# A third x tile turned on TensorE at the start, with the first columns of its z brought forward, in a gated mix of linear attention and a spatial MLP

## The chip, the core and the metric

One core of one Trainium2 chip. The metric is the time of one execution in microseconds (us), as the device measures it. A profile of one execution stands beside it: it gives the span from the first to the last instruction, which is a little shorter than the time.

## The reference

For x of 2048 rows and 512 columns the result is a mix of two branches by a gate for each row, all in bf16 with wide sums:

```python
g = _sigmoid((x * gate_w).sum(-1, keepdims=True))
a = _A_ref(x, A_wqkv, A_w_phi, A_wo)     # linear attention, softmax features, 32 heads of 16
b = _B_ref(x, B_w_in, B_w_sp, B_b_sp, B_w_out)
return g * a + (1 - g) * b

def _B_ref(x, w_in, w_sp, b_sp, w_out):
    z = _gelu(jnp.einsum('bsd,df->bsf', x, w_in))      # F = 1376 columns, d = 512
    z1 = z[..., :Fh].copy()
    z2 = _layernorm(z[..., Fh:], axis=-1)
    g = jnp.einsum('ts,bsf->btf', w_sp, z2) + b_sp[None, :, None]
    return jnp.einsum('bsf,fd->bsd', z1 * g, w_out)
```

The change lies in the very first part: x @ w_in, with gate_w carried as one more column of w_in, and the gelu behind it.

## The kernel before

The 2048 rows are 16 tiles of 128 rows. TensorE needs x with its 512 columns on the partitions, as four blocks dt of 128: that is `xT[:, dt, rows]`. For each tile t, z is 1377 columns (1376 of w_in and the gate's column F), done in three pieces, `Z_PIECES` = (0, 512), (512, 1024), (1024, 1377), each a sum over four blocks dt. The three pieces of a tile take three PSUM banks: 0 to 2 for even tiles, 3 to 5 for odd ones (`zbank`). ScalarE then applies gelu to all of the tile's columns in one activation (`z_post`), takes tanh of the gate column, and VectorE takes the layernorm's statistics. Banks 6 and 7 are left for other uses: value projections, the folding of weights, and, at the start, the turning of x.

The order of instructions on each engine is the order of the text (`manual_schedule`); no engine's instructions are reordered against it, and waits between engines come from the data. So the start of the kernel reads as follows.

- `spin(24)` (line 195) runs matmuls on constants into bank 5, while the first loads are on the way. Their results are not used.
- x tiles 0 and 1 are loaded as they are (`xn`, by SP's and ACT's queue), and turned by matmuls with an identity, `x_transpose` (line 201): four 128-column matmuls a tile, into bank 6 for tile 0 and bank 7 for tile 1. `x_copy` brings them from PSUM to `xT` in three parts, for tile 0 on VectorE (line 210), for tile 1 on ScalarE (line 212). `spin(4)` stands behind the transposes.
- w_in is loaded in pieces: columns 0 to 256 (HC) and 256 to 512, each split between SP's and ACT's queue; 512 to 1024 in two halves on SP's; then the rest on SP's. gate_w (`gw`) is loaded on ACT's queue, behind the pieces of w_in and ahead of a one-element gelu.
- z of tiles 0 and 1 is computed in turns of one block each, by columns 0 to 256, 256 to 512 and 512 to 1024. `gate_column` (lines 215 and 218) stands after column 512: a 4-column matmul turns gate_w, and VectorE writes it as column F of w_in. The third piece of both tiles follows.
- Tiles 2 to 15 follow in full, each with its three pieces. x of tiles 2 and 3 comes by one transposing DMA on SP's queue (line 128), of the other tiles by three more. From tile 5 on, projections of v and the folding of weights stand between the tiles.

All z matmuls have line 186. After tile 15 come the features of k and q, the matmuls with w_sp, and the output tiles; the change doesn't touch these.

Of the kernel before, what the change touches and what calls it, by code (L numbers as in the profile page):

```python
# [7 lines left out]
AF = mybir.ActivationFunctionType  # L8
# [3 lines left out]
BF16 = mybir.dt.bfloat16  # L12
I32 = mybir.dt.int32

P = 128
S = 2048
D = 512
H = 32
DH = 16
F = 1376  # L20
# [3 lines left out]
NDT = D // P  # L24
CH = 512
# [15 lines left out]
def kernel(  # L41
# [14 lines left out]
    nc = tc.nc  # L56
    x2 = A_x.flatten_outer_dims()
    out2 = out.flatten_outer_dims()

    pers = ctx.enter_context(tc.tile_pool(name="pers", bufs=1))  # L60
# [5 lines left out]
    ps = psp.tile([P, 8, CH], FP32, name="ps")  # L66

    def zbank(t):
        b = 3 * (t % 2)
        return ps[:, b:b + 3, :].rearrange("p b n -> p (b n)")  # L70

    xT = pers.tile([P, NDT, S], BF16, name="xT")
    w_in = pers.tile([P, NDT, F + 1], BF16, name="w_in")
# [6 lines left out]
    zz = pers.tile([P, NT, F], BF16, name="zz")  # L80
# [6 lines left out]
    wphi = pers.tile([P, NDT, P], BF16, name="wphi")  # L87
    mask16 = pers.tile([P, 8], BF16, name="mask16")
    mask4 = pers.tile([P, 4], BF16, name="mask4")
    xn = pers.tile([P, 2, D], BF16, name="xn")  # L90
    ones = nc.const_aps.tensor(1.0, [P, P], BF16)
    stats = pers.tile([P, NT, 2, 6], FP32, name="stats")
    mv = pers.tile([P, NT, 2], FP32, name="mv")
# [7 lines left out]
    gate = st[:, 2, :]  # L101
    gatem = st[:, 3, :]

    ident = pers.tile([P, P], BF16, name="ident")
    gw = pers.tile([NDT, P], BF16, name="gw")
    nc.gpsimd.memset(ident[:], 1.0)
    nc.gpsimd.affine_select(
        out=ident[:], in_=ident[:], pattern=[[-1, P]],
# [7 lines left out]
    def load_w_in(eng, d0, d1, n0, n1):  # L116
        eng.dma_start(out=w_in[:, d0:d1, n0:n1], in_=w_in_v[:, d0:d1, n0:n1])

    HC = CH // 2
    for n0 in (0, HC):  # L120
        load_w_in(nc.sync, 0, 2, n0, n0 + HC)
        load_w_in(nc.scalar, 2, 4, n0, n0 + HC)
    for d0 in (0, 2):
        load_w_in(nc.sync, d0, d0 + 2, CH, 2 * CH)
    nc.scalar.dma_start(out=gw[:], in_=gate_w.rearrange("(dt p) -> dt p", p=P))
    nc.scalar.activation(out=st[:, 9, 0:1], in_=ones[:, 0:1], func=AF.Gelu_apprx_tanh)
    nc.sync.dma_start(out=w_in[:, :, 2 * CH:F], in_=w_in_v[:, :, 2 * CH:F])
    nc.sync.dma_start_transpose(out=xT[:, :, 2 * P:CH], in_=x2[2 * P:CH, :])
    nc.sync.dma_start(
        out=wv[:, :, :],  # L130
        in_=A_wqkv[:, 2 * D:3 * D].rearrange("(dt p) n -> p dt n", p=P),
    )
    for q in range(1, NCH):
        nc.sync.dma_start_transpose(
            out=xT[:, :, q * CH:(q + 1) * CH], in_=x2[q * CH:(q + 1) * CH, :]
        )
        if q == 1:
            nc.sync.dma_start(
                out=wphiW[:, :, :],
                in_=A_w_phi.rearrange("(g h) e f -> (h e) g f", g=NDT),  # L140
# [3 lines left out]
        out=bcolb[:, :, :], in_=B_b_sp.rearrange("(t p) -> t p", p=P)  # L144
# [7 lines left out]
    for t in range(WSLOTS):  # L152
        load_wsp(t)
    nc.sync.dma_start(
        out=w_out[:, 0:NFT - 1, :],
        in_=B_w_out[0:(NFT - 1) * P, :].rearrange("(ft p) n -> p ft n", p=P),
# [4 lines left out]
        out=w_out[0:last_m, NFT - 1, :], in_=B_w_out[(NFT - 1) * P:FH, :]  # L161
    )
    nc.sync.dma_start(
        out=wo[:, :, :], in_=A_wo.rearrange("(g p) n -> p g n", p=P)
# [4 lines left out]
        out=mask16[:], in_=mask16[:], pattern=[[-16, 8]],  # L169
# [3 lines left out]
        out=mask16[:], in_=mask16[:], pattern=[[16, 8]],  # L173
# [6 lines left out]
    nc.gpsimd.memset(worst[:], 1.0)  # L180
    nc.vector.tensor_tensor(out=mask4[:], in0=mask16[:, 0:4], in1=mask16[:, 4:8], op=ALU.add)

    def z_piece(t, n0, n1, d0=0, d1=NDT):
        zb = zbank(t)
        for dt in range(d0, d1):
            nc.tensor.matmul(  # L186
                zb[:, n0:n1], lhsT=xT[:, dt, t * P:(t + 1) * P], rhs=w_in[:, dt, n0:n1],
                start=(dt == 0), stop=(dt == NDT - 1),
            )

    Z_PIECES = [(0, CH), (CH, 2 * CH), (2 * CH, F + 1)]

    def spin(n):
        for _ in range(n):
            nc.tensor.matmul(  # L195
                ps[:, 5, 0:P], lhsT=ones, rhs=ones, start=True, stop=True
            )

    def x_transpose(t):
        for dt in range(NDT):  # L200
            nc.tensor.matmul(  # L201
                ps[:, 6 + t, dt * P:(dt + 1) * P], lhsT=xn[:, t, dt * P:(dt + 1) * P],
                rhs=ident[:], start=True, stop=True,
            )

    def x_copy(t, d0, d1):
        src = ps[:, 6 + t, :].rearrange("p (d n) -> p d n", d=NDT)
        dst = xT[:, d0:d1, t * P:(t + 1) * P]
        if t == 0:
            nc.vector.tensor_copy(out=dst, in_=src[:, d0:d1, :])  # L210
        else:
            nc.scalar.activation(out=dst, in_=src[:, d0:d1, :], func=AF.Copy)

    def gate_column():
        nc.tensor.matmul(  # L215
            ps[:, 6, 0:NDT], lhsT=gw[:], rhs=ident[0:NDT, 0:NDT], start=True, stop=True
        )
        nc.vector.tensor_copy(out=w_in[:, :, F], in_=ps[:, 6, 0:NDT])

    def z_gelu(t, n0, n1):  # L220
        nc.scalar.activation(  # L221
            out=zz[:, t, n0:n1], in_=zbank(t)[:, n0:n1], func=AF.Gelu_apprx_tanh
        )

    def z_post(t, done=0):
        zb = zbank(t)
        z_gelu(t, done, F)
        nc.scalar.activation(out=gth[:, t:t + 1], in_=zb[:, F:F + 1], func=AF.Tanh, scale=0.5)
        for h in range(2):
            nc.vector.bn_stats(  # L230
                out=stats[:, t, h, :], in_=zz[:, t, FH + h * HF:FH + (h + 1) * HF]
            )
        nc.vector.bn_aggr(out=mv[:, t, :], in_=stats[:, t, :, :].rearrange("p h s -> p (h s)"))
# [43 lines left out]
    def z1_gate(t):  # L277
        nc.vector.tensor_scalar(
            out=zz[:, t, 0:FH], in0=zz[:, t, 0:FH],
            scalar1=gatem[:, t:t + 1], scalar2=None, op0=ALU.mult,  # L280
        )
# [3 lines left out]
    def v_proj(t):  # L285
        b = VBANK.get(t, 6 + t % 2)
        for dt in range(NDT):
            nc.tensor.matmul(  # L288
                ps[:, b, :], lhsT=xT[:, dt, t * P:(t + 1) * P], rhs=wv[:, dt, :],
                start=(dt == 0), stop=(dt == NDT - 1),  # L290
            )
        nc.scalar.activation(
            out=vv[:, t, :, 0:HW], in_=ps[:, b, :].rearrange("p (g n) -> p g n", g=NHG),
            func=AF.Copy,
        )

    def build_wphi():
        nc.vector.tensor_tensor(
            out=wphi[:].rearrange("p g (h f) -> p g h f", h=8),
            in0=wphiW[:, :, None, :].to_broadcast([P, NDT, 8, DH]),  # L300
            in1=mask16[:, None, :, None].to_broadcast([P, NDT, 8, DH]),
            op=ALU.mult,
        )

    def fold(j):
        qk, dt = divmod(j, NDT)
        dst = wk if qk == 0 else wq
        b = 6 + (j + 1) % 2
        off = 4 if qk == 0 else 0
        for kc in range(NDT):  # L310
            nc.tensor.matmul(  # L311
                ps[:, b, kc * P:(kc + 1) * P],
                lhsT=wqkT[:, off + kc, dt * P:(dt + 1) * P], rhs=wphi[:, kc, :],
                start=True, stop=True,
            )
        nc.scalar.activation(out=dst[:, dt, :], in_=ps[:, b, :], func=AF.Copy)
# [9 lines left out]

    def e_slot(i):
        if i == 5:
            flat = xn[:].rearrange("p t d -> p (t d)")
        else:  # L330
            flat = w_in_flat[:, i * 2 * D:(i + 1) * 2 * D]
        return flat.rearrange("p (g a n) -> p g a n", g=NHG, a=2)
# [51 lines left out]
    def k_proj(t, general=False):  # L384
        ek_t[t] = e_slot(t % 4)
        feat(t, wk, KBANK[t % 2], ek_t[t], general)
# [4 lines left out]
    def q_proj(t, general=False):  # L391
        eq_t[t] = e_slot(4 + t % 2 if t < 4 else (t - 4) % 6)
        feat(t, wq, QBANK[t % 2], eq_t[t], general)
# [129 lines left out]
    VLAG = 5  # L523
    spin(24)
    x_transpose(0)
    x_transpose(1)
    for d0, d1 in ((0, 1), (1, 2), (2, NDT)):
        x_copy(0, d0, d1)
        x_copy(1, d0, d1)
    spin(4)  # L530
    for n0, n1 in ((0, HC), (HC, CH), Z_PIECES[1]):
        for dt in range(NDT):
            z_piece(0, n0, n1, dt, dt + 1)
            z_piece(1, n0, n1, dt, dt + 1)
        if n1 == CH:
            z_gelu(0, 0, CH)
            gate_column()
    z_gelu(0, *Z_PIECES[1])
    z_piece(0, *Z_PIECES[2])
    z_post(0, done=2 * CH)  # L540
    z_piece(1, *Z_PIECES[2])
    z_post(1)
    build_wphi()
    for t in range(2, NT):
        for n0, n1 in Z_PIECES:
            z_piece(t, n0, n1)
        z_post(t)
        if t >= VLAG:
            v_proj(t - VLAG)
        if 5 <= t < 13:  # L550
            fold(t - 5)
        if t in (3, 7, 11):
            ln_batch(t - 3, t + 1)
        if t == 14:
            ln_batch(12, 15)
        if t == 7:
            nc.vector.tensor_copy(out=bcol[:], in_=bcolb[:, 0, :])
        if t >= 5:
            z1_gate(t - 5)
# [119 lines left out]
```

## Time and profile before

| | |
|---|---|
| median of 3 runs | 208.35 us (208.07 to 208.62) |
| time of the profiled execution | 208.31 us |
| its span | 206.6 us |
| TensorE matmuls busy | 202.8 us, 98% of the span |
| VectorE, ScalarE, GpSimd busy | 151.0, 80.4, 63.3 us |
| granted TensorE clock | 1.00 |
| first matmul, first z matmul | 0.84 us, 4.63 us from the span's start |
| first z matmul of tile 2, of tile 3 | 10.28 us, 12.61 us |

A matmul's busy time holds its run through the array too, so successive ones overlap: the distance from start to start says what one costs, the duration doesn't. In a line of the chain of waits stand the start, the length and what ran, all in us; in a group's line the count follows the x. PE is TensorE, PEld its loading of weights, DVE VectorE, ACT ScalarE, and SP the engine that issues most of the DMAs.

### The profile page before, as it was taken

How to read it: one execution, taken by the hardware profiler on the slowest of the kernel's cores; microseconds unless marked ns; L12 is line 12 of the kernel's file. 1: busy time of each engine (PE TensorE's matmuls, PEld its weight loads, DVE VectorE, ACT ScalarE, POOL GpSimd, SP SyncE). 2: the span in 40 equal slices, each digit the busy share in tenths (PEclk: the TensorE clock that was granted, in tenths of full speed). 3: DMA queues.
4: the chain of work that ended last, by engine and by line, in shares of the span. 5: the costliest groups of instructions: out<-in, count | busy, mean ns of one | idle time of the engine just before them, and what ended most of it. 6: DMA issues, size and time to landing. Idle time of an engine off the chain costs nothing.

```text
span 206.6 us, 3777 instructions
## 1 busy us (share of the span) xinstructions
PE 202.8 (98%) x1400; PEld 118.3 (57%) x1400; DVE 151.0 (73%) x310; ACT 80.4 (39%) x142; POOL 63.3 (31%) x79
## 2 busy tenths in 40 slices
PE   8999999999999999999999999999999999999994
PEld 8655555544455666666666667666455554555542
DVE  1059858285977888879797996798989779796512
ACT  4366767676684323251514101222534233241110
POOL 4000000000003464636474764053543363433000
PEclk9999999999999999999999999999999999999999
DMA  6999999994000635463777782135675965877451
GB/s 196 294 153 251 200 182 229 192 218 133 0 3 0 140 80 101 102 141 67 148 120 95 155 172 41 38 86 106 122 155 117 161 134 128 89 162 153 99 127 55
DMA packets 90384, 26.56 MB, mean 129 GB/s; under 512 B 84296, under 2 KB 90360, under 8 KB 90360
## 3 DMA queue, kind: packets, MB, share of 16 engines
q1 hardware_dynamic: 87648, 24.13, 59.0%
q10 hardware_dynamic: 2712, 2.13, 4.1%
q8 instruction: 12, 0.20, 0.4%
q14 instruction: 12, 0.10, 0.2%
HBM read 3.44 MB, written 2.10 MB: 27 GB/s over the span
## 4 chain that ended last, share of the span: by engine, by line
PE 98%; DVE 0%; ACT 0%; issue 0%; DVEq 0%
PE ps L435 36%; PE ps L186 18%; PE ps L335 13%; PE ps L494 10%; PE ps L288 7%; PE ps L499 7%; PE ps L473 2%; PE ps L407 2%; PE ps L195 2%; PE ps L311 1%; PE ps L201 0%; DVE ob L506 0%; ACT ob L508 0%; PE ps L215 0%; PE ps L461 0%
## 5 line engine op out<-in xcount | busy, mean ns | idle before, releaser
L435 PE MATMUL ps<-zz,wsp 128*128 128x344 bf16 x512 | 84.1, 309 | 0.0
L367 POOL TENSOR_TENSOR worst<-worst,zr 128x128 f32<-128x128 f32 x32 | 28.6, 894 | 124.4 <-DVE zr L365 117.3
L435 PEld LDWEIGHTS <-wsp 128*128 128x128 bf16 x512 | 49.8, 98 | 27.8
L343 ACT ACTIVATE w_in<-ps 128x512 bf16<-128x512 f32 x56 | 30.1, 596 | 63.4 <-POOL w_in L371 20.8
L186 PE MATMUL ps<-w_in,xT 128*128 128x512 bf16 (+2 forms) x200 | 40.0, 355 | 0.0
L364 DVE TENSOR_REDUCE zr<-w_in 128x64 f32<-128x1024 bf16 x28 | 33.8, 1208 | 0.0
L443 DVE SCALAR_TENSOR_TENSOR u<-ps,bcol,zz 128x344 bf16<-128x344 f32 x32 | 18.4, 574 | 20.0 <-PE ps L473 8.6
L186 PEld LDWEIGHTS <-xT 128*128 128x128 bf16 x200 | 19.4, 99 | 17.5
L371 POOL TENSOR_TENSOR w_in<-w_in,zr 128x512 bf16<-128x512 bf16 x28 | 29.4, 1050 | 0.0
L221 ACT ACTIVATE zz<-ps 128x1376 bf16<-128x1376 f32 (+2 forms) x18 | 21.4, 1190 | 18.5 <-PE ps L186 18.4
L230 DVE BATCH_NORM_STATS2 stats<-zz 128x6 f32<-128x344 bf16 x32 | 14.8, 505 | 12.0 <-ACT zz L221 12.0
L494 PE MATMUL ps<-w_out,uT 128*128 128x512 bf16 (+2 forms) x102 | 23.5, 367 | 0.0
L407 PE MATMUL ps<-vv,w_in 128*128 128x65 bf16 x128 | 21.7, 193 | 0.0
L371 DVE TENSOR_TENSOR w_in<-w_in,zr 128x512 bf16<-128x512 bf16 x28 | 19.4, 692 | 1.0
L508 ACT ACTIVATE ob<-ps 128x512 bf16<-128x512 f32 (+1 forms) x14 | 8.0, 574 | 27.0 <-PE ps L499 21.1
L365 DVE RECIPROCAL zr<-zr 128x64 f32<-128x64 f32 x32 | 17.7, 553 | 1.1
L499 PE MATMUL ps<-wo,oT 128*128 128x512 bf16 (+2 forms) x68 | 16.6, 367 | 0.0
L335 PEld LDWEIGHTS <-xT 128*128 128x128 bf16 x128 | 10.8, 98 | 9.9
L335 PE MATMUL ps<-wq,xT 128*128 128x512 bf16 x64 | 16.4, 379 | 0.0
L335 PE MATMUL ps<-wk,xT 128*128 128x512 bf16 x64 | 16.3, 379 | 0.0
L473 PE MATMUL ps<-kvx,wqkT 128*128 128x68 bf16 x128 | 15.8, 194 | 0.0
L288 PE MATMUL ps<-wv,xT 128*128 128x512 bf16 x64 | 15.6, 379 | 0.0
(64 smaller groups left out, 145.2 us busy)
## 6 DMA issues: line engine op xcount, KB each, us to landing
out_dram<-ob ACTq DMA_DIRECT2D x13, 128.0 KB, 2.7
w_out<-in_B_w_out_dram SPq DMA_DIRECT2D x1, 640.0 KB, 6.2
w_in<-in_B_w_in_dram SPq DMA_DIRECT2D x2, 256.0 KB, 3.7
wv<-in_A_wqkv_dram SPq DMA_DIRECT2D x1, 512.0 KB, 5.5
wo<-in_A_wo_dram SPq DMA_DIRECT2D x1, 512.0 KB, 6.4
w_in<-in_B_w_in_dram SPq DMA_DIRECT2D x1, 352.0 KB, 4.2
w_in<-in_B_w_in_dram ACTq DMA_DIRECT2D x2, 128.0 KB, 3.6
w_in<-in_B_w_in_dram SPq DMA_DIRECT2D x2, 128.0 KB, 3.1
```

Source lines behind the costliest of these rows:

```text
L186: nc.tensor.matmul(zb[:, n0:n1], lhsT=xT[:, dt, t * P:(t + 1) * P], rhs=w_in[:, dt, n0:n1], start=(dt == 0), stop=(dt == NDT - 1),)
L221: nc.scalar.activation(out=zz[:, t, n0:n1], in_=zbank(t)[:, n0:n1], func=AF.Gelu_apprx_tanh)
L288: nc.tensor.matmul(ps[:, b, :], lhsT=xT[:, dt, t * P:(t + 1) * P], rhs=wv[:, dt, :], start=(dt == 0), stop=(dt == NDT - 1),)
L335: nc.tensor.matmul(ps[:, b, :], lhsT=xT[:, dt, t * P:(t + 1) * P], rhs=w[:, dt, :], start=(dt == 0), stop=(dt == NDT - 1),)
L343: nc.scalar.activation(out=e[:, :, a, :], in_=src, func=AF.Exp, scale=sc)
L364: nc.vector.tensor_reduce(out=zs, in_=ev, axis=AX.X, op=ALU.add)
L367: nc.gpsimd.tensor_tensor(out=worst[:], in0=worst[:], in1=zr[:].rearrange("p a h -> p (a h)"), op=ALU.add)
L371: eng.tensor_tensor(out=ev[:, sl, :], in0=ev[:, sl, :], in1=rs[:, sl, None].to_broadcast([P, H, DH]), op=ALU.mult,)
L407: nc.tensor.matmul(slots[:, g, 0:HW + 1], lhsT=ek_t[t][:, g, :, :].rearrange("p a n -> p (a n)"), rhs=vv[:, t, g, 0:HW + 1], start=(t == 0 ...
L435: nc.tensor.matmul(ps[:, b, 0:HF], lhsT=wsp[:, tt % WSLOTS, s, :], rhs=zz[:, s, FH + h * HF:FH + (h + 1) * HF], start=(s == 0), stop=(s == ...
L494: nc.tensor.matmul(ps[:, b, n0:n1], lhsT=uT[:, ft, :], rhs=w_out[:, ft, n0:n1], start=(ft == 0), stop=False,)
L499: nc.tensor.matmul(ps[:, b, n0:n1], lhsT=oT[:, g, :], rhs=wo[:, g, n0:n1], start=False, stop=(g == NDT - 1),)
```

## The change

- `xn` has room for a third tile. Tile 2 of x is loaded into it on ACT's queue, between ACT's two pieces of w_in. The transposing DMA on SP's queue then brings tile 3 alone.
- The load of gate_w moves on ACT's queue from behind the pieces of w_in to behind `x_copy`. `spin(4)` becomes `spin(3)`.
- After columns 0 to 256 of z for tiles 0 and 1, tile 2 is turned on TensorE into bank 7, and VectorE copies it to `xT` in two parts. Columns 0 to 256 of tile 2's z follow, into bank 6; then columns 256 to 512 of tiles 0 and 1, then the same columns of tile 2.
- `gate_column` uses bank 7, and stands in the middle of the piece 512 to 1024 of tiles 0 and 1.
- The gelu of tile 2's first 512 columns is an activation of its own, after tile 1's; when tile 2's turn comes, only its second and third pieces are computed.

```diff
-    xn = pers.tile([P, 2, D], BF16, name="xn")
+    xn = pers.tile([P, 3, D], BF16, name="xn")
...
         load_w_in(nc.scalar, 2, 4, n0, n0 + HC)
+        if n0 == 0:
+            nc.scalar.dma_start(out=xn[:, 2, :], in_=x2[2 * P:3 * P, :])
     for d0 in (0, 2):
         load_w_in(nc.sync, d0, d0 + 2, CH, 2 * CH)
-    nc.scalar.dma_start(out=gw[:], in_=gate_w.rearrange("(dt p) -> dt p", p=P))
     nc.scalar.activation(out=st[:, 9, 0:1], in_=ones[:, 0:1], func=AF.Gelu_apprx_tanh)
     nc.sync.dma_start(out=w_in[:, :, 2 * CH:F], in_=w_in_v[:, :, 2 * CH:F])
-    nc.sync.dma_start_transpose(out=xT[:, :, 2 * P:CH], in_=x2[2 * P:CH, :])
+    nc.sync.dma_start_transpose(out=xT[:, :, 3 * P:CH], in_=x2[3 * P:CH, :])
...
+    XBANK = (6, 7, 7)
+
     def x_copy(t, d0, d1):
-        src = ps[:, 6 + t, :].rearrange("p (d n) -> p d n", d=NDT)
+        src = ps[:, XBANK[t], :].rearrange("p (d n) -> p d n", d=NDT)
         dst = xT[:, d0:d1, t * P:(t + 1) * P]
-        if t == 0:
+        if t != 1:
             nc.vector.tensor_copy(out=dst, in_=src[:, d0:d1, :])
...
-    spin(4)
-    for n0, n1 in ((0, HC), (HC, CH), Z_PIECES[1]):
+    nc.scalar.dma_start(out=gw[:], in_=gate_w.rearrange("(dt p) -> dt p", p=P))
+    spin(3)
+    zb2 = ps[:, 6, :]
+
+    def z_pair(n0, n1, gate=False):
         for dt in range(NDT):
+            if gate and dt == 2:
+                gate_column()
             z_piece(0, n0, n1, dt, dt + 1)
             z_piece(1, n0, n1, dt, dt + 1)
-        if n1 == CH:
-            z_gelu(0, 0, CH)
-            gate_column()
+
+    z_pair(0, HC)
+    x_transpose(2)
+    x_copy(2, 0, 1)
+    x_copy(2, 1, NDT)
+    z_piece(2, 0, HC, zb=zb2)
+    z_pair(HC, CH)
+    z_gelu(0, 0, CH)
+    z_piece(2, HC, CH, zb=zb2)
+    z_pair(*Z_PIECES[1], gate=True)
     z_gelu(0, *Z_PIECES[1])
     z_piece(0, *Z_PIECES[2])
     z_post(0, done=2 * CH)
     z_piece(1, *Z_PIECES[2])
     z_post(1)
+    z_gelu(2, 0, CH, zb2)
     build_wphi()
     for t in range(2, NT):
-        for n0, n1 in Z_PIECES:
+        for n0, n1 in Z_PIECES[1 if t == 2 else 0:]:
             z_piece(t, n0, n1)
-        z_post(t)
+        z_post(t, done=CH if t == 2 else 0)
```

More of the change, by code (lines that the diff above doesn't have):

```diff
@@ L181, with z_piece @@
     nc.vector.tensor_tensor(out=mask4[:], in0=mask16[:, 0:4], in1=mask16[:, 4:8], op=ALU.add)
-    def z_piece(t, n0, n1, d0=0, d1=NDT):
-        zb = zbank(t)
+    def z_piece(t, n0, n1, d0=0, d1=NDT, zb=None):
+        zb = zbank(t) if zb is None else zb
         for dt in range(d0, d1):
@@ L201, in x_transpose @@
             nc.tensor.matmul(
-                ps[:, 6 + t, dt * P:(dt + 1) * P], lhsT=xn[:, t, dt * P:(dt + 1) * P],
+                ps[:, XBANK[t], dt * P:(dt + 1) * P], lhsT=xn[:, t, dt * P:(dt + 1) * P],
                 rhs=ident[:], start=True, stop=True,
@@ L215, in gate_column, with z_gelu @@
         nc.tensor.matmul(
-            ps[:, 6, 0:NDT], lhsT=gw[:], rhs=ident[0:NDT, 0:NDT], start=True, stop=True
+            ps[:, 7, 0:NDT], lhsT=gw[:], rhs=ident[0:NDT, 0:NDT], start=True, stop=True
         )
-        nc.vector.tensor_copy(out=w_in[:, :, F], in_=ps[:, 6, 0:NDT])
-    def z_gelu(t, n0, n1):
+        nc.vector.tensor_copy(out=w_in[:, :, F], in_=ps[:, 7, 0:NDT])
+    def z_gelu(t, n0, n1, zb=None):
+        zb = zbank(t) if zb is None else zb
         nc.scalar.activation(
-            out=zz[:, t, n0:n1], in_=zbank(t)[:, n0:n1], func=AF.Gelu_apprx_tanh
+            out=zz[:, t, n0:n1], in_=zb[:, n0:n1], func=AF.Gelu_apprx_tanh
         )
@@ L328, in e_slot @@
         if i == 5:
-            flat = xn[:].rearrange("p t d -> p (t d)")
+            flat = xn[:, 0:2, :].rearrange("p t d -> p (t d)")
         else:
```

## The prediction

> **What bounds the kernel now.** I read the page's busy shares and chain first, then the chain of waits for the first 24 us, because the whole change lies there.
>
> ```profile
> PE 202.8 (98%) x1400; PEld 118.3 (57%) x1400; DVE 151.0 (73%) x310; ACT 80.4 (39%) x142; POOL 63.3 (31%) x79
> ...
> PE 98%; DVE 0%; ACT 0%; issue 0%; DVEq 0%
> ```
>
> TensorE is the chain. So the time changes by what the change adds to or takes from TensorE's own sequence, and by nothing else unless another engine becomes late. The chain of the first 24 us (start, length, what) says where a gain could come from:
>
> ```profile
> 0.84 2.72 PE ps L195 x24
> 3.56 0.85 PE ps L201 x8
> 4.41 0.43 PE ps L195 x4
> 4.84 2.46 PE ps L186 x16
> 7.29 0.10 PE ps L215
> 7.40 12.37 PE ps L186 x64
> ```
>
> From the first real z matmul on there is no DMA, no copy and no "issue" in it: no piece of w_in and no piece of xT is waited for. That is the main reading, since loading a third x tile and starting its z early can only pay where TensorE would else stand still. What looks like slack at the start is a slow clock. The groups of line 186 in 4.6 to 6.1 us and in 6.27 to 7.2 us (durations min/median/max):
>
> ```profile
> L186 PE MATMUL ps<-w_in,xT x7: 395/421/421, 4.6 to 5.9; 128*128 128x256 bf16 x7
> ...
> L186 PE MATMUL ps<-w_in,xT x10: 270/273/395, 5.9 to 7.0; 128*128 128x256 bf16 x10
> ```
>
> The first eight 256-column matmuls follow each other every 213 ns (4.63 to 6.13), the next every 109 ns. The granted clock reads 1.00 in both stretches, so the page's PEclk row doesn't show this; the spacing does. Of the 2.46 us of those sixteen, 8 x 0.104 = 0.83 us is the slow clock, and the rest is the work.
>
> Two more places matter for what the change adds. The first is the existing turn of an x tile: transposes, copies, z (timeline):
>
> ```profile
> 3.35 1.06 PE L201 MATMUL ps<-ident,xn 128*128 128x128 bf16 x8
> 4.02 0.82 DVE L210 CAST xT<-ps 128x128 bf16<-128x128 f32 x3 [1.43 <-PE ps L201]
> 4.45 0.72 ACT L212 ACTIVATE xT<-ps 128x128 bf16<-128x128 f32 x3
> ```
>
> Today the time from the matmuls to the copies is covered: x_copy(0) runs under the transposes of tile 1, and x_copy(1) under spin(4). The second is a naked wait of TensorE for VectorE, late in the kernel:
>
> ```profile
> 189.49 0.16 DVE L456 TENSOR_SCALAR safeb<-worst 128x1 bf16<-128x1 f32 x1
> 189.72 0.08 PEld L461 LDWEIGHTS <-safeb 128*1 128x1 bf16 x1 [0.42 <-DVE safeb L456]
> ```
>
> From the end of the DVE instruction (189.65) to the weight load it is 0.07 us.
>
> **The change part by part.** The sum is against the profiled execution, 208.31 us: span 206.6 and 1.7 around it, which nothing here touches. The median is 208.35, so I count from either.
>
> *One spin fewer.* A 128-column spin takes 0.107 us on the slow clock. But z of tile 1 can't start before x_copy(1)'s first part, 4.45 + 0.28 = 4.73, plus some 0.05; today it starts at 4.85. So at most 0.07 us is gained, and on the half-speed clock half of that is real work: -0.03 (0 to -0.1).
>
> *x_transpose(2), four matmuls.* New on TensorE. Four 128-column matmuls of line 311 take 0.22 us on the fast clock (20.63 to 20.85); the eight of line 201 took 0.85, so four on the slow clock 0.43. z_pair(0, HC) ends near 6.2, where the clock opened: +0.22 (to 0.43). The DMA transpose that this replaces cost TensorE nothing: tile 2's z begins at 10.28 without a wait.
>
> *The wait for x_copy(2).* This is the big term. In the written order z_piece(2, 0, HC) follows the transposes at once, and everything of TensorE is queued behind it: z_pair(HC, CH), which needs nothing of tile 2, and all later tiles. Count from the start of the last transpose, t. It ends at t + 0.22 (a 128-column matmul on the fast clock, 203.20 0.22 in the timeline). x_copy starts 0.04 later, as 4.02 against the fourth transpose's end at 3.99; it waited for all four though it reads one quarter, for DVE was idle. The first 128-column copy takes 0.29: t + 0.55. Weights 0.07 later: t + 0.62, where without a wait the next matmul starts at t + 0.06. First stall: 0.56. Then one matmul of 0.11, to t + 0.73. The second copy starts 0.2 after the first (4.02, 4.23, 4.43 today), and is 384 columns: 128 took 0.28 and 256 took 0.41, so 384 some 0.54. It ends near t + 1.0, weights at t + 1.07. Second stall: 0.34. Together +0.9. Below: if the copies start after the first transpose, 0.17 less. Above: on the slow clock the first link is 0.1 longer. It can't be below nothing, since TensorE has no wait there now that it could replace. If the clock is still slow during all this, the stall costs half, since it uses up slow time: then +0.45.
>
> *z of tile 2 split and moved.* Its 512 columns are done as 2 x 256: 8 x 0.1095 instead of 4 x 0.2165 us, +0.01. Moving them is otherwise neutral.
>
> *Tile 3 behind a shorter tile 2.* Tile 2 now has 1377 - 512 = 865 columns left after tile 1, 0.87 + 0.60 = 1.47 us of matmuls. Tile 3's first piece writes the bank that tile 1's gelu reads. That gelu starts 0.35 after tile 1's last matmul (10.48 against 10.13) and takes 1.32, to 1.67; tile 3 would reach it at 0.15 + 1.47 = 1.62. With the 0.05 to 0.07 of a semaphore that is +0.1 (0 to 0.15). Before, the full 2.33 us of tile 2 covered it.
>
> *Loads.* xn's tile 2 goes on ACT's queue ahead of the second w_in piece: 128 KB at the 335 to 357 GB/s that the windows of this stretch show is 0.37 us for what follows. The pieces have the slack: the ACT half of HC to CH lands at 1.73 + 3.6 = 5.3 and is first used at 6.7, 512 to 1024 lands by 6.9 and its second half is used at 8.2, the rest lands at 7.9 and is used at 9.1; and all uses are now 0.9 to 1.6 us later. Cost nothing; if w_in came 1.3 us late, TensorE would wait for the difference.
>
> *gate_w later.* Its issue (0.62 us of ACT's queue) leaves the place before the table load, where xn's issue (0.41) stands in; it now follows x_copy(1) and is out by 5.8. Behind it waits z_gelu(0), not due before 8.7. Its landing isn't shown; with the 2.3 to 4.2 us of other loads it is 7.5 to 9.4, and gate_column now comes near 10. The gate matmul itself breaks the stream by 0.2 us as now (7.02 to 7.33 for what would be 0.11), only in another place. VectorE's copy then has four matmuls of cover, 0.87 us against 0.3. Nothing.
>
> *SP's queue.* Its x transpose has 128 rows instead of 256, so of 1.35 us of issue about half goes, and wv and all behind it start 0.6 earlier. Nobody waits for these. Also gelu(2) as two activations costs ACT about 0.1; ACT idles 0.95 before each tile's gelu.
>
> Sum: -0.03 + 0.22 + 0.9 + 0.01 + 0.1 = +1.2 us, so 209.5. With the stall and the transposes all on the slow clock it is 0.45 + 0.22 + 0.1 = +0.75, 209.1; with every upper end +1.6, 209.9.
>
> **Rivals.**
>
> *The clock opens later.* The new wait makes TensorE idle 0.9 us in the very stretch in which the clock opened. For: the slow stretch lasted 5.4 us from the first matmul (0.84 to 6.2), so something must be met before it ends. Against: by order of the code the wait begins after 6.2. It decides if the clock is still slow when the wait begins. Each us of slow clock costs half a us; a further 2 to 5.4 us slow is +1 to +2.7: 210.5 to 212.2. [...]
>
> *The clock opens earlier.* If the time of the opening varies between executions and falls at the first z matmul, the 0.83 us of the slow eight is saved: 209.5 - 0.8 = 208.7, within 0.3%. For: nothing in the code fixes it. Against: the three times of before lie within 0.55 us.
>
> *The wait is covered after all (not slower).* If w_in's HC to CH came so late that z_pair(HC, CH) couldn't start before 7.8 anyway, tile 2's turn and z would fill a hole that the kernel already has. Price: stall and transposes drop out, leaving +0.1, and below that what was waited for before: 208.0 to 208.4. It decides from a landing 1.3 us later than the 5.3 of this trace. Against it is the chain, with no wait for a DMA, and a time that agrees with the median.
>
> **How the numbers follow.** The forecast has 0.78, with its own range 208.9 to 210.0. Later clock 0.06, earlier clock 0.09, covered wait 0.07. A difference of 0.3% (0.63 us), about what a measurement of this kernel can tell from no change, means under 207.72 or over 208.98. Faster: half of the covered case, 0.04. Same: the rest of it, the earlier clock, and a little of the forecast's low end, 0.13. Slower: 0.83. The range 208.6 to 210.3 leaves out the covered wait and most of the late clock.
>
> **What would show it.** Right: in the chain of the first 24 us, two gaps of TensorE ended by DVE's x_copy, about 0.55 and 0.35 us, between four more L201-like matmuls and z of tile 2; tile 3's z starting near 13.8 instead of 12.6; no wait for w_in; everything after shifted by the same amount. Wrong: a w_in wait in the changed trace that swallows the gaps, z_pair running before z_piece(2), or the 213 ns spacing ending at another time than 6.2.

## The result, and the profile after

The changed kernel takes 212.22 us (210.53 to 214.63, 6 runs), beside 208.52 for the kernel before (208.07 to 208.70, 6 runs): slower, ratio 1.0153 with an interval of 1.0115 to 1.019. Two of the six, 214.19 and 214.63, had a mean granted clock of 0.992 and 0.991 where the others had 0.998 or more, and they stand in the median but not in the ratio. The direction was forecast, but the time lies 1.9 us above the upper end of the range. The profiled execution took 211.65 us, 3.34 more than that of before.

Busy shares and chain of the changed kernel:

```profile
PE 202.1 (96%) x1384; PEld 118.3 (56%) x1407; DVE 151.8 (72%) x312; ACT 80.4 (38%) x143; POOL 63.4 (30%) x79
...
PE 92%; DMA 5%; issue 1%; SPq 1%; DVE 0%; ACT 0%; DVEq 0%
```

TensorE's busy time is nearly the same (202.1 us, before 202.8), and 5% of the chain is now DMA, which before had no place in it. The chain of waits of the first 24 us (start, length, what) says which DMAs:

```profile
2.22 5.12 DMA w_in<-in_B_w_in_dram
7.34 0.02 issue
7.36 4.84 DMA gw<-in_gate_w_dram
12.20 0.04 issue
12.25 0.17 PE ps L218
12.42 8.84 PE ps L187 x46
```

It is read backwards. The z matmuls wait for the gate matmul (line 218), this for gate_w, 1 KB, which took 4.84 us from its issue at 7.36 to its landing. The issue itself waited for a piece of w_in that landed at 7.34. No data goes from that piece to gate_w; what goes over is a semaphore. In the trace both loads have number 108: the last of that piece's sixteen landing events on it is at 7.34, and gate_w's issue, whose record names a wait for 108 and no other, starts at 7.36. In the traces of both kernels the program's loads use eight numbers in turn (100 and 102 to 108), and in the first 40 us each one from the ninth on waits for the number that it takes, so for the load eight before it on the list. In the kernel before, gate_w was among the first eight (107, issued at 2.27) and had none to wait for. The ninth was SP's fourth piece of w_in, the last of the four in the second row here (issued at 3.29), and it waited on 100 for ACT's xn (third row: issued at 0.80, landed 2.5 us later, at 3.27):

```profile
2.27 0.62 ACTq L125 DMA_DIRECT2D gw<-in_gate_w_dram  x1
...
L117 SPq DMA_DIRECT2D w_in<-in_B_w_in_dram x4: 368/438/469, 1.3 to 3.3; - x4
...
xn<-in_A_x_dram ACTq DMA_DIRECT2D x1, 128.0 KB, 2.5
```

TensorE's waits in the first 20 us (total, times, longest):

```profile
PE ps L218 <- DMA gw<-in_gate_w_dram: 1.5, 1, 1.5
...
PE ps L204 <- DMA xn<-in_A_x_dram: 0.8, 1, 0.8
...
PE ps L187 <- DVE xT L213: 0.6, 2, 0.5
```

And the same stretch in order of time:

```profile
4.58 1.45 PE L187 MATMUL ps<-w_in,xT 128*128 128x256 bf16 x8
...
6.03 0.57 SPq L130 DMA_DIRECT2D wv<-in_A_wqkv_dram  x1
6.75 4.42 SPq L135 DMA_TRANSPOSE xT<-in_A_x_dram  x1
...
6.78 0.40 PE L204 MATMUL ps<-ident,xn 128*128 128x128 bf16 x4 [0.75 <-DMA xn<-in_A_x_dram]
7.29 0.76 DVE L213 CAST xT<-ps 128x128 bf16<-128x128 f32 x2 [2.39 <-PE ps L204]
7.36 0.52 ACTq L534 DMA_DIRECT2D gw<-in_gate_w_dram  x1
...
7.64 0.28 PE L187 MATMUL ps<-w_in,xT 128*128 128x256 bf16 x1 [0.46 <-DVE xT L213]
8.10 2.19 PEld L187 LDWEIGHTS <-xT 128*128 128x128 bf16 x19 [0.37 <-DVE xT L213]
8.10 2.68 PE L187 MATMUL ps<-w_in,xT 128*128 128x256 bf16 x18 [0.18 <-DVE xT L213]
...
12.25 0.17 PE L218 MATMUL ps<-ident,gw 4*128 4x4 bf16 x1 [1.47 <-DMA gw<-in_gate_w_dram]
```

The brackets count idle time from the modelled end of the matmul before. What a wait costs is the distance from start to start beyond what the matmul needs; the account below uses that. Where z of tile 3 starts, 16.00 us against 12.61, all of the loss is already there.

| step (start to start, profiled executions) | predicted | measured |
|---|---|---|
| one spin fewer, and the clock: z_pair(0, HC) done at 5.86 against 6.26 | -0.03 | -0.39 |
| wait for the third x tile, which landed at 6.73 | 0 | +0.92 |
| four transposes | +0.22 | +0.23 |
| waits for the two copies | +0.56, +0.34 | +0.62, +0.35 |
| wait of the gate matmul, beyond the 0.2 of before | 0 | +1.53 |
| tile 3's wait for its bank | +0.1 | +0.10 |
| sum | +1.2 | +3.36 |

The start of tile 3's z moved by 3.39 and the time by 3.34. In this execution the clock opened at 5.4 us instead of 6.15, by the trace's clock record, which hid 0.35 of the loss.

### The profile page after: what moved, and what is told of

Read it like the earlier page. It is cut to its first block, busy times and chain, and to the rows that moved or that the text cites. A ratio compares the mean times of both kernels' runs of the same rounds, so it can differ in the third digit from the quotient of the medians.

```text
span 209.9 us, 3772 instructions
## 1 busy us (share of the span) xinstructions
PE 202.1 (96%) x1384; PEld 118.3 (56%) x1407; DVE 151.8 (72%) x312; ACT 80.4 (38%) x143; POOL 63.4 (30%) x79
## 3 DMA queue, kind: packets, MB, share of 16 engines
HBM read 3.57 MB, written 2.10 MB: 27 GB/s over the span
## 4 chain that ended last, share of the span: by engine, by line
PE 92%; DMA 5%; issue 1%; SPq 1%; DVE 0%; ACT 0%; DVEq 0%
PE ps L439 36%; PE ps L187 16%; PE ps L339 13%; PE ps L498 10%; PE ps L292 7%; PE ps L503 6%; DMA w_in<-in_B_w_in_dram 2%; DMA gw<-in_gate_w_dram 2%; PE ps L477 2%; PE ps L411 2%; PE ps L315 1%; SPq L117 0%; DVE ob L510 0%; SPq L113 0%; ACT ob L512 0%
## 5 line engine op out<-in xcount | busy, mean ns | idle before, releaser
L225 ACT ACTIVATE zz<-ps 128x1376 bf16<-128x1376 f32 (+3 forms) x19 | 21.4, 1138 | 21.9 <-PE ps L187 21.8
L339 PEld LDWEIGHTS <-xT 128*128 128x128 bf16 x128 | 10.8, 98 | 9.9
L339 PE MATMUL ps<-wk,xT 128*128 128x512 bf16 x57 | 15.7, 379 | 0.3
L339 PE MATMUL ps<-wq,xT 128*128 128x512 bf16 x57 | 15.6, 379 | 0.3
```

The costliest lines, as they stand in the source:

```text
L225: nc.scalar.activation(out=zz[:, t, n0:n1], in_=zb[:, n0:n1], func=AF.Gelu_apprx_tanh)
L339: nc.tensor.matmul(ps[:, b, :], lhsT=xT[:, dt, t * P:(t + 1) * P], rhs=w[:, dt, :], start=(dt == 0), stop=(dt == NDT - 1),)
```

## The experiments

The first theory: three separate waits (gate_w, the third tile's landing, its copies). The rival: the turning of the tile is the loss, and what is saved on one wait is lost on the next.

**gate_w back at its old place.**

```diff
+    nc.scalar.dma_start(out=gw[:], ...)
     nc.scalar.activation(out=st[:, 9, 0:1], in_=ones[:, 0:1], func=AF.Gelu_apprx_tanh)
...
-    nc.scalar.dma_start(out=gw[:], ...)
     spin(3)
```

> The changed kernel with one thing undone: gate_w is loaded at its old place, on ACT's queue behind the pieces of w_in and ahead of the table load. Theory (three separate waits of TensorE, by the trace of the changed kernel: 1.5 us for gate_w, 0.9 us for the third x tile, 1.0 us for its copies, plus 0.23 us of transposes and 0.1 us at tile 3): the gate matmul no longer waits, the time falls by about 1.5 us against the changed kernel, to 210.1 to 210.8, still 1.6 to 2.3 over before; the spread between runs shrinks too. Rival (the loss is the turn of tile 2 and the disturbed clock, and gate_w's wait only stands in for a wait that then appears elsewhere, such as for w_in's third piece): the time stays within 0.4 us of the changed kernel.

Measured: 211.52 us (209.90 to 213.28), ratio 1.0148 (1.0092 to 1.0205). By the median neither was right: it is 0.7 us under the changed kernel, where the theory asked for about 1.5 and the rival for at most 0.4, and the spread did not shrink. The profiled execution, 210.11, lies where the theory had it. ScalarE's part of the timeline, and TensorE's new wait:

```profile
3.74 0.52 ACTq L127 DMA_DIRECT2D gw<-in_gate_w_dram  x1
4.29 1.28 ACT L128 ACT_TABLE_LOAD   x1 [4.29 <-DMA xn<-in_A_x_dram]
...
5.69 0.70 ACT L216 ACTIVATE xT<-ps 128x128 bf16<-128x128 f32 x3
```

```profile
PE ps L188 <- ACT xT L216: 0.9, 1, 0.9
```

The wait for gate_w is gone, and a wait for x_copy(1) has come in the place of that for the third tile: the tile's transposes start at 6.79 us here and at 6.78 in the changed kernel, so this execution is faster by gate_w's wait alone (211.65 to 210.11). With the third x tile on the list, the load of gate_w here is issued at 3.74 instead of 2.27, behind the landing of xn (the profile puts ACT's wait down to it), and ACT's row (its instructions in their order) stands still behind it: the table load of 1.28 us, on the line of the one-element gelu, starts at 4.29 instead of 2.92, x_copy(1) at 5.69 instead of 4.45. So in these runs the added load has a price wherever the ninth load of the list is issued by an engine that has work behind it. Three of the six runs lie near 210.1, where the theory had them, and three near 212.9; the profiled one is of the lower group. What parts them stays open: the granted clock is 0.999 or more in all six, but it reads 1.00 before the opening too, so it doesn't tell whether the clock opened later in the upper three.

**Only gate_w's move, in the kernel before.**

```diff
-    nc.scalar.dma_start(out=gw[:], ...)      # behind the pieces of w_in
...
+    nc.scalar.dma_start(out=gw[:], ...)      # behind x_copy
     spin(4)
```

> The kernel before with one thing done: gate_w's load moved on ACT's queue behind x_copy, nothing else. Theory (the late load is dear by itself: it waits for a semaphore that an earlier load must give back, and then its transfer stands behind SP's transposing DMA): the gate matmul, due at 7.1 us here, waits for a landing between 8.5 and 12.2, so 1.3 to 5 us slower than before, 209.8 to 213.5, all of it one gap before the gate matmul. Rival (the move is free where nothing else is changed): 208.2 to 208.8.

Measured: 214.07 us (211.89 to 214.74), ratio 1.0256 (1.0214 to 1.0297), 0.6 above the upper end. TensorE's wait, and windows of 4 us (us, PE busy, granted clock, DMA share, GB/s):

```profile
PE ps L214 <- DMA gw<-in_gate_w_dram: 4.2, 1, 4.2
```

```profile
8.00:12.00 4.00, 0.81 (x4) 0.95 1.15 296
12.00:16.00 4.00, 4.00 (x16) 0.62 0.97 198
16.00:20.00 4.00, 4.00 (x22) 1.00 1.48 238
```

The move alone is enough to lose 5.6 us. Here the gate matmul is due near 6.7 us, so a landing near 11 costs 4.2. And the clock went to half right after the gap, from 11.6 to 15.0 us by the trace's clock record, which is an estimated 1.7 us more (half of 3.4): sixteen matmuls fill the window from 12 to 16 us, and 22 the next. Five of the six runs have a mean granted clock of 0.984 to 0.992; the one at 1.00 took 211.89, which is 3.4 us over before.

**Tile 2's turn one piece later, and the same with the copies covered.** Both have gate_w at its old place, so both keep the wait for x_copy(1), and differ in the covering and, with it, in the place of the gate matmul.

```diff
 # later                                # later and covered
 z_pair(0, HC)                          z_pair(0, HC)
+z_pair(HC, CH)                         z_pair(HC, CH)
 x_transpose(2); x_copy(2, ...)         x_transpose(2); x_copy(2, ...)
-z_pair(HC, CH)                        +z_pair(*Z_PIECES[1]); gate_column()
 z_piece(2, 0, HC); z_piece(2, HC, CH)  z_piece(2, 0, HC); z_piece(2, HC, CH)
```

> Changed kernel with gate_w at its old place, and tile 2's transposes, copies and first 512 columns of z all placed behind columns 256 to 512 of tiles 0 and 1. The third x tile has then 0.9 us more to land, but the copies are as bare as in the changed kernel. Theory: the wait for the load is gone (or under 0.2 us), the two gaps for the copies stay at 0.6 and 0.35 us; with 0.23 us of transposes and 0.1 at tile 3 this is 0.9 us less than with gate_w's place alone undone, 209.4 to 209.9. Rival (the load's wait and the copies' wait are one thing, and what is saved on one is lost on the other): no less than with gate_w alone undone.

> As the run before, but columns 512 to 1024 of tiles 0 and 1 and the gate matmul stand between tile 2's copies and its z, so that both the load and the copies have other matmuls over them. Theory: what is left is the transposes (0.23 us) and tile 3's wait for the bank (0.1 us), less the spin (up to 0.07): 208.6 to 208.9, within 0.2% of before. Rival (turning a tile on TensorE costs beyond the waits, for instance by the split of z or ScalarE's extra gelu): over 209.4.

Measured: 210.27 us (209.87 to 211.90, ratio 1.0105, 1.0073 to 1.0137) and 209.12 us (208.93 to 209.91, ratio 1.0048, 1.0029 to 1.0066). All the waits of TensorE's matmuls between 1 and 20 us, of the first and then of the second:

```profile
PE ps L188 <- ACT xT L216: 0.9, 1, 0.9
...
PE ps L188 <- DVE xT L214: 0.6, 2, 0.5
PE ps L188 <- DMA w_in<-in_B_w_in_dram: 0.2, 1, 0.2
```

```profile
PE ps L188 <- ACT xT L216: 1.1, 1, 1.1
```

Put later, the turn has no wait for its load any more, though that tile landed at 6.58 us. With other matmuls over the copies their wait is gone as well, and the time falls by 1.15 us, of which the two gaps in the trace (0.62 and 0.36) are 0.98. Both times lie above what was expected, by 0.4 and 0.2 us, and the covered one between the theory and its rival. The large wait that the theory lacked is that for x_copy(1).

**gate_w among the first eight loads,** in the changed order and in the covered one.

```diff
             nc.scalar.dma_start(out=xn[:, 2, :], in_=x2[2 * P:3 * P, :])
+            nc.scalar.dma_start(out=gw[:], ...)
...
-    nc.scalar.dma_start(out=gw[:], ...)
     spin(3)
```

> The changed kernel with gate_w's load on ACT's queue right behind the third x tile, so that it is among the first eight loads, and the ACT half of w_in's second piece is behind it. Theory (in the run with gate_w at its old place the load was the ninth, waited for the semaphore of an earlier one until 3.7 us, and held ScalarE's table load and x_copy(1) behind it, which cost TensorE 0.9 us; among the first eight it holds nobody): no wait for x_copy(1) and none for gate_w; left are the copies (1.0 us), the third tile's landing (0 to 0.9), transposes and bank (0.35): 209.6 to 210.7, at least 0.7 under the run with gate_w at its old place. Rival (the place of x_copy(1) is set by the table load or by xn's landing, not by the ninth load): 211 to 212.

> gate_w among the first eight loads, and tile 2's transposes behind columns 256 to 512, its z behind columns 512 to 1024 and the gate matmul. Theory: every wait that the change brought is gone, what is left is 0.23 us of transposes and 0.1 us for the bank at tile 3: 208.6 to 208.9. Rival (turning a tile on TensorE early gains something once its waits are covered): under 208.2.

Measured: 209.88 us (209.72 to 210.12, ratio 1.0074, 1.0062 to 1.0086) and 209.53 us (209.32 to 210.75, ratio 1.0067, 1.0046 to 1.0088). The first met its range, for the wrong reason: x_copy(1) is waited for 1.2 us here. The ninth load of the list is now the second piece of w_in on ACT's row, issued at 3.57 when xn had landed, and the table load stands behind it. That piece also lands later (7.45 to 7.65), and the covered order, 0.6 us above its range, waits 0.4 us for it and 0.8 for x_copy(1). That is as the rival of the first experiment had it: one wait given for another.

**The loads mended.** Both pieces of w_in first on ACT's row, then the third x tile, the table load, and gate_w; in the changed and in the covered order.

```diff
         load_w_in(nc.scalar, 2, 4, n0, n0 + HC)
-        if n0 == 0:
-            nc.scalar.dma_start(out=xn[:, 2, :], ...)
+    nc.scalar.dma_start(out=xn[:, 2, :], ...)
...
     nc.scalar.activation(out=st[:, 9, 0:1], ..., func=AF.Gelu_apprx_tanh)
+    nc.scalar.dma_start(out=gw[:], ...)
...
-    nc.scalar.dma_start(out=gw[:], ...)
     spin(3)
```

> The changed kernel with only the order of ACT's loads mended: both pieces of w_in, then the third x tile, then the table load, then gate_w. TensorE's order is the changed one. So the first eight loads hold no engine, gate_w is issued by 4.6 us, ahead of the 512 KB of wv, and x_copy(1) isn't behind it. Theory: neither gate_w nor x_copy(1) is waited for; the copies (0.98 us), transposes and bank (0.33) and 0 to 0.7 for the third tile's landing are left: 209.6 to 210.4. Rival (the ninth load still holds ACT past 4.5 us): a wait for x_copy(1) of 0.8 to 1.2 us and 210.5 or more.

> The same loads, and tile 2's transposes behind columns 256 to 512, its z behind columns 512 to 1024 and the gate matmul. Theory: no wait is left but the bank at tile 3; 0.23 + 0.10 - 0.05 us over before, 208.6 to 208.9 and within 0.3% of it; TensorE's chain has no DMA and no copy in the first 24 us. Rival (each wait that is covered turns up elsewhere, as it did for the loads): 209.2 or more.

Measured: 210.38 us (210.19 to 213.70, ratio 1.0093, 1.0078 to 1.0108) and 208.80 us (208.49 to 209.29, ratio 1.0016, 1.0000 to 1.0032). Gate_w is not waited for in the first. But it was issued only at 4.6, again behind the landing of an earlier load (ACT's wait for a piece of w_in, 0.9 us, ends just before x_copy(1)), and x_copy(1) behind it cost 0.8 us, as that rival said; the time met the theory's range all the same. The second is the best form of the change: its only wait beyond tile 3's bank is 0.4 us for x_copy(1), and it is 1.6 us faster than the bare order with the same loads.

```profile
PE ps L187 <- ACT xT L215: 0.4, 1, 0.4
```

**gate_w on SP's row,** ahead of the transposing DMA, where no other engine's work is behind it; in both orders.

```diff
+    nc.sync.dma_start(out=gw[:], ...)
     nc.sync.dma_start_transpose(out=xT[:, :, 3 * P:CH], in_=x2[3 * P:CH, :])
...
-    nc.scalar.dma_start(out=gw[:], ...)
```

> The changed kernel with one line on another queue: gate_w is loaded on SP's queue, behind w_in's last piece and ahead of the transposing DMA. Nothing of ACT waits for a load's semaphore any more (in the run with mended loads gate_w still held x_copy(1) for 0.8 us). Theory: no wait for x_copy(1), none for gate_w; left are the copies (0.98 us), the third tile's landing (0 to 0.9), transposes and bank (0.33), less 0.05: 209.6 to 210.4, which is 1.5 us or more under the changed kernel. Rival (behind 1.3 MB of w_in gate_w comes too late on SP's queue also): a wait before the gate matmul of over 0.5 us and 210.8 or more.

> The same, with tile 2's transposes behind columns 256 to 512 and its z behind columns 512 to 1024 and the gate matmul. Theory: no wait is left but the bank at tile 3: before + 0.23 + 0.10 - 0.05, 208.5 to 208.8, equal or up to 0.3 below the run with mended loads and the same order. Rival (that run's 0.4 us wait for x_copy(1) was hidden by the slow clock and cost nothing): no difference to it, and 208.8 or more.

Measured: 209.63 us (208.88 to 212.00, ratio 1.0052, 1.0035 to 1.0068) and 209.06 us (208.84 to 209.70, ratio 1.0038, 1.0025 to 1.0050). The first is what the theory asked for: TensorE's order is wholly that of the changed kernel, one line stands on another queue, and the ratio falls from 1.0153 to 1.0052, some 2.1 us. Of these 1.53 are gate_w's wait in the changed kernel's trace; where the rest comes from stays open. In this run's trace neither gate_w nor x_copy(1) is waited for beyond 0.15 us; the third tile costs 1.13 and the copies 0.98, from start to start. The covered one missed its range by 0.3 us: the second piece of w_in, behind the third tile on ACT's row, landed at 7.12 and was waited for, 0.43 us from start to start, and the clock opened at 6.2, late.

The profiled run of the first is its slowest (212.00). Its windows:

```profile
4.00:8.00 4.00, 2.57 (x22) 1.00 1.02 302
8.00:12.00 4.00, 3.82 (x19) 0.57 1.25 252
12.00:16.00 4.00, 4.00 (x23) 1.00 1.00 188
```

0.57 over 4 us is half speed for 3.4 us; the six other runs at a mean clock of 0.998 or more take 208.88 to 209.81. In that stretch the matmuls of 256 columns follow each other every 213 ns (8.46 to 11.24), as the first ones of before do, so that spacing is half speed. The changed kernel's runs at 214.19 and 214.63 fit one such closing each, since 1.7 of 212.7 us is a mean clock of 0.992; a trace of them there is not. TensorE stood idle for 2.1 of the 3.4 us before the clock closed (5.04 to 8.45: 1.13 for the tile, 0.62 and 0.36 for the copies).

**What held gate_w's packets.** In the changed kernel its issue ended at 7.88, and its four packets ran at 11.4 to 11.8. Either SP's transposing DMA (6.75 to 11.17) held them, or the data issued ahead of them. Two plain loads, moved from the end of SP's row ahead of that DMA, were to tell the two apart:

```diff
     nc.sync.dma_start(out=wv[:, :, :], ...)
+    nc.sync.dma_start(out=w_out[:, 0:NFT - 1, :], ...)      # 640 KB
+    nc.sync.dma_start(out=wo[:, :, :], ...)                 # 512 KB
     for q in range(1, NCH):
         nc.sync.dma_start_transpose(out=xT[:, :, q * CH:(q + 1) * CH], ...)
```

> The changed kernel, gate_w's load left where the change put it; on SP's queue two plain loads (w_out's and wo's, 640 and 512 KB, at the end of the row in the changed kernel) stand ahead of the transposing DMAs of x. Theory (gate_w's four packets were not served until SP had issued the whole transposing DMA, 6.75 to 11.17 us, though its own issue ended at 7.88): with plain loads in that place gate_w lands before 10.5, and the gate matmul's wait of 1.5 us shrinks to under 0.5, so about 1 us or more faster than the changed kernel, unless x's later tiles, which come 3.4 us later, are waited for at tile 4 or at the first fold. Rival (the packets wait for the amount of data in front of them on the same 16 DMA engines): 1.15 MB more in front makes it later still, the wait grows to 2 us or more.

Measured: 212.24 us (211.98 to 214.03), ratio 1.0195 (1.0173 to 1.0217). The issues, and the wait:

```profile
6.51 0.50 SPq L134 DMA_DIRECT2D w_out<-in_B_w_out_dram  x1
7.05 1.34 SPq L138 DMA_DIRECT2D wo<-in_A_wo_dram  x1
7.26 0.52 ACTq L534 DMA_DIRECT2D gw<-in_gate_w_dram  x1
8.43 5.90 SPq L142 DMA_TRANSPOSE xT<-in_A_x_dram  x1
```

```profile
PE ps L218 <- DMA gw<-in_gate_w_dram: 2.8, 1, 2.8
```

My theory fell: the packets ran at 11.3 to 12.3, while SP was still issuing the transposing DMA behind them (8.43 to 14.33), and gate_w landed at 13.0. The wait grew past 2 us, as the rival had it, but by 1.3 us, of which 0.8 are the later landing; the rest is that the gate matmul was due 0.5 us earlier, since the clock opened at 3.6 here. Gate_w landed beside w_out (13.2), which SP had issued 0.75 us earlier, and ahead of wo (14.6), whose issue began 0.2 us earlier. In the changed kernel it landed at 12.2, beside wv (11.5), issued 1.3 us earlier, and in the run with gate_w's move alone at 11.0, beside wv (10.8). So in these three traces a small load on ACT's row lands at about the time of the large one that SP issued some 0.6 to 1.3 us ahead of it, though the two rows are different queues (q10 and q1 in the traces of before and after). A plain count of the bytes in front doesn't give it: 640 KB more, at the 300 GB/s of that stretch, would be an estimated 2.2 us, and the landing moved by 0.8. What decides it isn't settled by these runs.

**A try at a faster kernel.** From the kernel before, with the gate matmul in the place of spins:

```diff
     nc.scalar.dma_start(out=xn[:, 1, :], in_=x2[P:2 * P, :])
+    nc.scalar.dma_start(out=gw[:], ...)
...
-    nc.scalar.dma_start(out=gw[:], ...)      # behind the pieces of w_in
...
-    spin(4)
+    spin(2)
+    gate_turn()       # the 4-column matmul into bank 5; its copy stays behind column 512
```

> The kernel before, with gate_w loaded second on ACT's queue and its 4-column matmul done in the place of two of the four spins, into bank 5; VectorE's copy stays where it was. In the kernel before this matmul breaks the stream of z by 0.2 us (7.02 to 7.33 where 0.11 was due). Theory: that 0.2 us is saved, since the stretch in which it now runs is filled with spins anyway: 208.2 to 208.4, 0.1% faster. Rival (the load ahead of w_in delays the first piece, or the copy that waits for w_in's last piece is late): 208.5 or more.

Measured: 208.73 us (208.12 to 209.20), ratio 1.0013 (1.0001 to 1.0026): no gain, as the rival said. The matmul left the stream of z, but ACT's first w_in piece, now behind gate_w, was waited for 0.8 us. No version here beats the kernel before.

## Why the prediction was wrong

- **Held:** the kernel's bound, and that no wait was there to be filled; transposes, copies and bank within 0.1 us each; the direction.
- **Failed, "gate_w later ... Nothing":** the largest term, 1.53 us in the profile. Two steps of it were wrong. Its issue was to be over by 5.8, behind x_copy(1); it began at 7.36 and was over at 7.88, because the load waited for the semaphore of a piece of w_in that landed at 7.34. That could be read from the trace of before: SP's fourth piece of w_in starts at 3.29, just as xn lands at 3.27. And the landing was bounded by 7.5 to 9.4, from the 2.3 to 4.2 us that other loads took; it was 4.84 us after the start of its issue, with 512 KB of wv issued ahead of it, so 12.20 where the gate matmul was due at 10.6. The first step is shown by the semaphore in the chain; why the second takes so long stays open, as said above.
- **Failed, "Loads":** I gave the added tile's delay to w_in's pieces (0.37 us, covered), but never asked when the tile itself lands. Issued where the change put it, it landed between 5.4 and 6.9 us in these traces, and TensorE wanted it at 5.9 in the changed kernel's and at 5.8 in that with gate_w on SP's row, where it waited 0.92 and 1.13 us.
- **Taken too lightly, the clock rival (0.06):** it expected a late opening. None of the fourteen traces has one: by their clock records the clock opened between 3.5 and 6.2 us, in the kernel before at 6.15. What three of them have is a closing, half speed for 3.41 us each time, and 2 of the 6 runs of the changed kernel fit one. In the run with gate_w on SP's row the clock closed with TensorE idle for 2.1 of the 3.41 us before (from start to start). What decides on an opening or a closing, no run shows.
- **The earlier clock (0.09)** came in part: the 213 ns spacing ended at 5.4 us instead of 6.2, which the prediction had named as a sign of being wrong. It hid 0.35 us, far less than the two waits that were missing.
- **The covered wait** of the rivals did not occur: no z matmul of the changed kernel waited for w_in, and none of the gaps was filled.

By size: the forecast of +1.2 us is about what is left when the gate's load is taken out of the way (209.63, ratio 1.0052, so +1.1). That is partly luck: the trace of that run has 1.13 us of wait for the third tile, which the forecast put at nothing, beside a clock that opened 1.1 us earlier than before's.

## What to carry to other kernels

When a load is added or moved, count its place in the list of loads: here gate_w's load, waiting for an earlier one's semaphore, held all that stood behind it on its engine (at its old place x_copy(1) started at 5.69 us instead of 4.45), and with its 1 KB it landed about when the large one issued ahead of it did (12.2 beside 11.5 in the changed kernel). Put a small load that feeds the critical engine ahead of the large ones that are needed later, not of those needed sooner (gate_w ahead of w_in cost 0.8 us of wait), and on an engine with nothing behind it (on SP's row the ratio fell from 1.0153 to 1.0052). A tile that is turned on TensorE needs other matmuls over its copies (here 1.0 us bare, nothing visible when covered), and TensorE had no hole to fill: the best of these versions just about broke even with before (1.0016, 1.0000 to 1.0032).

## What was unexpected of the hardware

- 1 KB issued on ACT's queue took 4.84 us to land behind 512 KB on SP's, and its four packets ran within half a us at the end of that time (11.4 to 11.8, landing at 12.2).
- The clock closed for 3.41 us in the traces where TensorE had been idle for 2.1 (gate_w on SP's row), 2.6 (plain loads first) and 2.9 (gate_w's move alone) of the 3.41 us before, counted from start to start; it stayed open in the changed kernel's trace, with 1.9 of such a stretch idle. Half speed for 3.41 us is an estimated loss of up to 1.7 us, and the run with gate_w's move alone lost 5.6 us for a gap of 4.2: here a gap at the start cost more than its length.
